# Attention and a gated MLP in one kernel: nine score tiles a pair in three groups, the remainder tile transposed as one block, minimum and exponential over two banks

## The chip, the cores and the metric

The kernel runs on one core of a Trainium2 chip. The metric is the device time of one execution in microseconds (us), the median over runs. The core's engines are TensorE (PE in the rows; PEld is its weight load), VectorE (DVE), ScalarE (ACT), GpSimd (POOL) and SyncE (SP), which here only issues DMAs.

## The reference, cut to what matters

```python
q, k, v: (4, 8, 1152, 64) float32        # batch, heads, sequence, head size
q_pool = q.reshape(B, H, S // 2, 2, D).mean(axis=3)      # 576 queries a head
scores = matmul(q_pool, k.T) / sqrt(D)
scores = scores - max(scores); attn = exp(scores); attn = attn / (sum(attn) + 1e-9)
x = (attn @ v), heads side by side                        # (2304, 512)
g = x @ w_gate; out = (g * sigmoid(g) * (x @ w_val)) @ w_out    # hidden size 1536
```

The weights come as float64. Operands of products are split into a high and a low half (each exact in TensorE's fp32r form), so a product of two operands is taken in two or three parts.

## The kernel before, in words

The attention works on 16 pairs of heads, one after another, with the operands of a pair prepared one pair ahead. A head has 576 queries: four tiles of 128 (`QT`) and a remainder of 64 (`QR`). The remainders of a pair's two heads make one tile together, so a pair has nine score tiles (`NTILE`), each 128 queries by 1152 keys.

- **Scores** (`s_tile`, L411). A tile's keys come in three chunks of 384 columns. A chunk takes two products (L427; the remainder tile four, since its queries of both heads stand in one tile `qrt` with zeros in the other head's place) into one of four single banks `sc`. VectorE takes the minimum of the negated scores, the first chunk by a reduction (L433), the other two by `tensor_scalar` with an accumulator that starts from the chunk before (L435). ScalarE then takes three exponentials (L441), each with its sum, into `pn` (for the remainder tile `pnr`), and frees the bank.
- **Groups** (`group`, L526, and `unit`, L468). The exponentials are transposed on TensorE (L484), 128 keys by 128 queries at a time, so that the products with v contract over keys. Each head has two groups: its first two tiles (256 queries, two key chunks to a bank `pt`), and its last two with its 64 rows of the remainder tile (320 queries, one key chunk to a bank, the 64-row block first). The bank is split in a high and a low half: ScalarE casts (L499), VectorE subtracts (L503). In three of nine units of the second group the bank is copied out (L489, L491) and GpSimd does the split (L497, L503). Then come the products with v (L511), high and low, of 256 or 320 columns, into `po`. `evac` (L546) adds up the halves of the result.
- **Operands.** `prep` (L386) transposes the split k and q of the next pair (L393) and copies them out (L398, L400). Queries are needed as [high, low] and as [low, high]; the second is the first, moved across partitions by two DMAs of `swap` (L376): for head 0 (`qt0`), head 1 (`qt1`) and the remainder (`qrt`, one buffer).
- **Sums.** When all nine tiles of a pair have their sums, `total` (GpSimd) and `recip` (VectorE, L573) give the reciprocals `rc`; `spread` stores them to DRAM (`rs`, L581 and L582), and then loads them back, a copy in each of 64 rows (`rb`, L586). `norm` (L593) multiplies.

All DMAs of a pair are issued by SP, in one fixed order; an issue whose source isn't ready holds up those behind it. The order on every engine is laid down before the run: `Plan` (L78) takes instructions with a cost, a place in the program (in units of a score tile) and the buffers that they take and give, and lists each engine's instructions by its own arithmetic, in which the places are shifted by a table of numbers (`SHIFTS`, L34). The chip then runs each engine's list in that order, with semaphores. The banks are `sc` 4, `pt` 3, `po` 1, which is all eight.

The MLP behind it takes blocks of 384 tokens; its weights are decoded from float64 by ScalarE, VectorE and GpSimd while the first two blocks run.

## Time and profile before

| what | value |
|---|---|
| three runs | 1144.87, 1134.54, 1147.23 us; median 1144.87 |
| the profiled execution | span 1150.8 us; no other time of it is listed |
| TensorE | 1078.2 us busy (94% of the span), 6369 products and transposes |
| VectorE | 724.6 us busy (63%) |
| ScalarE | 633.2 us busy (55%) |
| GpSimd | 415.5 us busy (36%) |
| first MLP product | 668.4 us from the span's start |

The table gives averages over two stages: the attention up to 668 us, and the MLP. What an edit of the attention is worth is read from the first stage alone. A TensorE product's busy time overlaps the next one's, so that what a product takes of the engine is the distance from its start to the next one's start, or its share in the chain of waits. The same holds for VectorE and ScalarE, whose rows overlap by some 0.1 us.

### The profile page before, as it was taken

Reading aid. Unit: us, or ns where it says so; the run is one execution under the profiler, and the core shown is the slowest. Engines: PE = TensorE matmul, PEld = TensorE weight load, DVE = VectorE, ACT = ScalarE, POOL = GpSimd, SP = SyncE. Lnnn points to the kernel's source line nnn. Section 1 sums busy time; section 2 is a strip of 40 time slices with the busy share of each in tenths; the row PEclk is TensorE's granted clock in tenths of the full one; section 3 lists DMA queues with packets and bytes.
Section 4 is the critical chain, followed back from the end, with each engine's and each line's share of the span. In section 5 each row is a group of like instructions: output and inputs, shape, how many; then the busy total and the mean of one; then the engine's idle time right before and its main releaser. Section 6 shows DMA issues by size and latency. Waiting matters only on the chain.

```text
span 1150.8 us, 18611 instructions
## 1 busy us (share of the span) xinstructions
PE 1078.2 (94%) x6369; PEld 955.8 (83%) x6369; DVE 724.6 (63%) x1618; ACT 633.2 (55%) x1710; POOL 415.5 (36%) x494
## 2 busy tenths in 40 slices
PE   6989999999999999999999988889999999999997
PEld 4878887787888888778788877778999999999997
DVE  7877876777777787677777859997332322322221
ACT  6867877777787787777778844443121121211211
POOL 7465446646447644644643244442110100100000
PEclk9999999999999999999999999999999999999999
DMA  6333134223224213312312024441020110100101
GB/s 219 106 103 80 49 106 122 40 80 97 56 61 133 77 32 105 96 37 80 77 35 34 22 76 146 147 146 38 28 83 1 28 29 1 55 1 1 28 1 28
DMA packets 68478, 77.17 MB, mean 67 GB/s; under 512 B 24032, under 2 KB 44384, under 8 KB 68384
## 3 DMA queue, kind: packets, MB, share of 16 engines
q1 hardware_dynamic: 68208, 75.59, 23.8%
q8 instruction: 50, 0.82, 0.3%
q14 instruction: 44, 0.36, 0.2%
q0 software_dynamic: 96, 0.26, 0.1%
q10 hardware_dynamic: 80, 0.13, 0.0%
HBM read 56.62 MB, written 9.51 MB: 57 GB/s over the span
## 4 chain that ended last, share of the span: by engine, by line
PE 72%; DVE 11%; ACT 6%; DMA 6%; issue 4%; SPq 0%; POOL 0%; POOLq 0%; DVEq 0%; ACTq 0%
PE pg L770 20%; PE pt L484 16%; PE sc L427 14%; PE po L511 10%; PE pa L792 10%; ACT pn L441 3%; DMA qrt<-qrt 3%; DVE wa L240 3%; PE pt L393 2%; DVE junk L435 2%; DVE w L244 2%; ACT ph L499 1%; DVE wa L236 1%; DVE sg L778 1%; DVE pl L503 1%
## 5 line engine op out<-in xcount | busy, mean ns | idle before, releaser
L770 PE MATMUL pg<-x,wh 128*128 128x384 f32 x1152 | 295.3, 337 | 0.0
L441 ACT ACTIVATE pn<-sc,mx 128x384 f32<-128x384 f32 x384 | 225.1, 591 | 4.6 <-DVE junk L435 3.1
L435 DVE TENSOR_SCALAR_CACHE_REDUCE junk<-sc,mx 128x384 f32<-128x384 f32 x288 | 177.6, 617 | 74.7 <-PE sc L427 65.3
L427 PE MATMUL sc<-kt,qt 128*128 128x384 f32 x768 | 213.6, 363 | 7.2 <-ACT pn L441 7.1
L484 PE MATMUL pt<-ident,pn 128*128 128x128 f32 x1152 | 215.0, 292 | 3.0 <-DVE pl L503 3.0
L770 PEld LDWEIGHTS pg<-x,wh 128*128 128x128 f32 x1152 | 208.8, 188 | 5.7
L770 PE MATMUL pg<-x,wl 128*128 128x384 f32 x576 | 194.8, 338 | 19.0 <-DVE sg L778 18.8
L778 DVE TENSOR_TENSOR sg<-pg,sg 128x384 f32<-128x384 f32 x144 | 80.0, 556 | 208.8 <-ACT sg L775 124.2
L503 DVE TENSOR_TENSOR pl<-pt,ph 128x320 fp32r<-128x320 f32 (+2 forms) x352 | 191.4, 551 | 8.5 <-ACT ph L499 7.3
L499 ACT CAST ph<-pt 128x320 fp32r<-128x320 f32 (+2 forms) x352 | 166.5, 483 | 47.7 <-PE pt L484 41.1
L511 PE MATMUL po<-ph,vs 128*128 128x256 f32 (+1 forms) x576 | 180.3, 326 | 0.0
L511 PE MATMUL po<-pl,vs 128*128 128x256 f32 (+1 forms) x576 | 164.6, 299 | 0.0
L484 PEld LDWEIGHTS pt<-ident,pn 128*128 128x128 f32 x1152 | 133.1, 144 | 27.1 <-DVE pl L503 2.5
L770 PEld LDWEIGHTS pg<-x,wl 128*128 128x128 f32 x576 | 108.7, 189 | 32.1 <-DVE sg L778 14.8
L427 PEld LDWEIGHTS sc<-kt,qt 128*128 128x128 f32 x768 | 120.7, 191 | 13.2 <-ACT pn L441 12.3
L782 ACT CAST hh<-sg 128x384 fp32r<-128x384 f32 x72 | 36.9, 513 | 152.3 <-PE pa L792 137.7
L511 PEld LDWEIGHTS po<-ph,vs 128*128 128x128 f32 x576 | 110.6, 192 | 1.0
L511 PEld LDWEIGHTS po<-pl,vs 128*128 128x128 f32 x576 | 111.1, 193 | 0.3 <-DVE pl L503 0.3
L433 DVE TENSOR_REDUCE mx<-sc 128x1 f32<-128x384 f32 x144 | 79.5, 552 | 49.3 <-PE sc L427 44.9
L775 ACT ACTIVATE sg<-pg 128x384 f32<-128x384 f32 x72 | 35.3, 490 | 126.3 <-PE pg L770 121.8
L427 PE MATMUL sc<-kt,qrt 128*128 128x384 f32 x192 | 57.1, 433 | 31.0 <-DMA qrt<-qrt 30.0
L792 PE MATMUL pa<-wh,hh 128*128 128x512 f32 x216 | 85.7, 397 | 0.0
(72 smaller groups left out, 1537.6 us busy)
## 6 DMA issues: line engine op xcount, KB each, us to landing
vraw<-in_v_dram SPq DMA_DIRECT2D x16, 576.0 KB
kraw<-in_k_dram SPq DMA_DIRECT2D x15, 576.0 KB
qraw<-in_q_dram SPq DMA_DIRECT2D x15, 512.0 KB
qt<-qt SPq DMA_DIRECT2D x60, 128.0 KB
wraw<-in_moe_w_out_dram SPq DMA_DIRECT2D x12, 512.0 KB
wraw<-in_moe_w_val_dram SPq DMA_DIRECT2D x12, 512.0 KB
wraw<-in_moe_w_gate_dram SPq DMA_DIRECT2D x12, 512.0 KB
rb<-rs SPq DMA_DIRECT2D x32, 144.0 KB
```

The source lines that it names most:

```text
L427: nc.tensor.matmul(cell[n][:, 0:KW], lhsT=lhsT, rhs=s[f"kt{jj}"][:, n * KW:(n + 1) * KW], start=(m == 0), stop=(m == len(terms) - 1))
L433: nc.vector.tensor_reduce(mx[:, 0:1], src, axis=AX.X, op=ALU.min)
L435: nc.vector.tensor_scalar(junk, src, mx[:, n - 1:n], None, op0=ALU.min, op1=ALU.min, accum_out=mx[:, n:n + 1])
L441: nc.scalar.activation(s["p", i][:, n * KW:(n + 1) * KW], cell[n][:, 0:KW], AF.Exp, bias=cell["mx"][:, 2:3], scale=-1.0, accum_out=s["sums ...
L484: nc.tensor.transpose(cell["ps"][:, o:o + r], s["p", i][r0:r0 + r, c * P:(c + 1) * P], ident[r0:r0 + r, r0:r0 + r])
L499: nc.scalar.copy(cell["h"][:, 0:w], cell["ps"][:, 0:w])
L503: e.tensor_sub(cell["l"][:, 0:w], cell["f" if kind else "ps"][:, 0:w], cell["h"][:, 0:w])
L511: nc.tensor.matmul(o[:, 0:n], lhsT=s["vs"][:, j, c, :], rhs=cell[x][:, a * n:(a + 1) * n], start=(first and a == 0 and x == "h"), stop=(en ...
L770: nc.tensor.matmul(o[:, 0:TB], lhsT=a[:, i, ws], rhs=b, start=(n == 0), stop=(n == 3 * NC - 1))
L778: nc.vector.tensor_mul(cell["s"], cell[i][:, 0:TB], cell["s"])
L782: nc.scalar.copy(cell["h"], cell["s"])
L792: nc.tensor.matmul(acc[blk, t], lhsT=cell[a][:, t * P:(t + 1) * P], rhs=b[:, 2, :], start=(f == 0 and n == 0), stop=(f == NF - 1 and n == 2),)
```

## The change

The score tile's three single banks become a bank pair `sa` (chunks 0 and 1, one slot) and a single bank `sb` (chunk 2, two slots). Chunk 2's products come first and are reduced; then chunks 0 and 1 are filled, and one VectorE instruction takes the minimum of both, and one ScalarE instruction their exponential; a second, short exponential follows for chunk 2. The nine tiles are taken in three groups of three: three of head 0; head 0's last, the remainder tile and one of head 1; three of head 1. A unit is one key chunk of a group, three transposes into one bank of 384 columns. In the middle group the remainder tile is transposed whole, and its two heads' 64 columns are written to two places in the bank, so that each head's 192 columns lie side by side; the products with v are then two pairs of 192 columns there, and one pair of 384 in the other groups. GpSimd takes no more part in the split. `Plan` has new costs for TensorE, and the table of shifts is new. In the changed kernel L431 are the score products, L488 the transposes of exponentials, L390 those of operands, L504 the products with v, L439 the two-bank minimum, L447 the exponentials, L373 the swaps, L563 and L564 the store and L568 the spreading of the reciprocals.

```diff
-        banks = {"sc": 4, "pt": 3, "po": 1}
+        banks = {"sa": 1, "sb": 2, "pt": 3, "po": 1}
...
-            "pn": 6, "pnr": 2, "ph": 5, "xs": 1, "tmp": 1, "pf": 2, "rb": 1, "xf": 1, "sums": 2, "rc": 2, "mx": 4,
+            "pn": 8, "ph": 5, "xs": 1, "tmp": 1, "rb": 1, "xf": 1, "sums": 2, "rc": 2, "mx": 4,
...
-            t = op({"PE": 0.056 * n}, pos, tr, after=after, take=("pt", *take), give=give, load=-1)
+            t = op({"PE": 0.065 * n}, pos, tr, after=after, take=("pt", *take), give=give, load=-1)
...
-            return (None, None) if i == QT else (1, i - QT - 1)
+            return (None, None) if i == QT else (1, (i - QT - 2) % QT)
...
             def mms(n):
+                if n == 2:
+                    cell["mx"] = new("mx", [P, 2], F32)
+                    cell["b"] = bank("sb", [P, 512])
                 if n == 0:
-                    cell["mx"] = new("mx", [P, 3], F32)
-                cell[n] = bank("sc", [P, 512])
+                    cell["a"] = bank("sa", [P, 2, 512])
+                o = cell["b"] if n == 2 else cell["a"][:, n]
...
             def low(n):
-                mx, src = cell["mx"], cell[n][:, 0:KW]
+                mx = cell["mx"]
                 if n == 0:
-                    nc.vector.tensor_reduce(mx[:, 0:1], src, axis=AX.X, op=ALU.min)
+                    nc.vector.tensor_reduce(mx[:, 0:1], cell["b"][:, 0:KW], axis=AX.X, op=ALU.min)
                 else:
-                    nc.vector.tensor_scalar(junk, src, mx[:, n - 1:n], None, op0=ALU.min, op1=ALU.min, accum_out=mx[:, n:n + 1])
+                    nc.vector.tensor_scalar(junk, cell["a"][:, :, 0:KW], mx[:, 0:1], None, op0=ALU.min, op1=ALU.min, accum_out=mx[:, 1:2])
 
             def exp(n):
...
                 nc.scalar.activation(
-                    s["p", i][:, n * KW:(n + 1) * KW], cell[n][:, 0:KW], AF.Exp, bias=cell["mx"][:, 2:3], scale=-1.0,
-                    accum_out=s["sums"][:, n, i:i + 1],
+                    o[:, 0:2 * KW].rearrange("p (a k) -> p a k", a=2) if n == 0 else o[:, 2 * KW:S],
+                    cell["a"][:, :, 0:KW] if n == 0 else cell["b"][:, 0:KW], AF.Exp, bias=cell["mx"][:, 1:2], scale=-1.0,
+                    accum_out=s["sums"][:, n, c:c + 1],
                 )
...
+            w = 0.175 * len(terms)
+            a, x = None, None
+            after = [*ready[2], *([done["s", p, m] for m in range(i)] if give else [])]
+            a = op({"PE": w}, pos - 0.3, lambda: mms(2), after=after, take=("sb", "mx"), load=1)
+            x = op({"DVE": 0.47}, pos - 0.25, lambda: low(0), after=[a])
+            a = op({"PE": w}, pos, lambda: mms(0), after=[a, *ready[0]], take=("sa",), load=1)
+            a = op({"PE": w}, pos + 0.01, lambda: mms(1), after=[a, *ready[1]], give=give, load=1)
+            x = op({"DVE": 0.95}, pos + LOW_AT, lambda: low(1), after=[a, x], more=0.04)
+            done["s", p, i] = a
+            x = op({"ACT": 0.88}, pos + EXP_AT, lambda: exp(0), after=[x], take=("pn", "sums") if i == 0 else ("pn",), give=("sa",))
+            done["p", p, i] = op({"ACT": 0.56}, pos + EXP_AT + 0.01, lambda: exp(1), after=[x], give=("sb", "mx"))
...
+        GROUPS = [
+            ([(0, None), (1, None), (2, None)], [(0, 0, 3 * P, 0)]),
+            ([(3, 0), (4, None), (5, P + QR)], [(0, 0, P + QR, 3 * P), (1, P + QR, 2 * (P + QR), 3 * P)]),
+            ([(6, None), (7, None), (8, None)], [(1, 0, 3 * P, 0)]),
+        ]
+        GW = 3 * P
...
+                for m, (i, o) in enumerate(tiles):
+                    src = s["p", i][:, c * P:(c + 1) * P]
+                    if i == QT:
+                        dst = cell["ps"][:, 0:GW].rearrange("p (a n) -> p a n", a=2)[:, :, P:P + QR]
+                        nc.tensor.transpose(dst, src, ident.rearrange("p (a n) -> p a n", a=2))
+                    else:
+                        o = m * P if o is None else o
+                        nc.tensor.transpose(cell["ps"][:, o:o + P], src, ident)
...
+                for n, (j, c0, c1, _) in enumerate(heads):
                     for x in ("h", "l"):
                         nc.tensor.matmul(
-                            o[:, 0:n], lhsT=s["vs"][:, j, c, :], rhs=cell[x][:, a * n:(a + 1) * n],
-                            start=(first and a == 0 and x == "h"), stop=(end and a == len(cs) - 1 and x == "l"),
+                            o[:, c0:c1], lhsT=s["vs"][:, j, c, :], rhs=cell[x][:, c0:c1],
+                            start=(c == 0 and n == 0 and x == "h"), stop=(c == KC - 1 and x == "l"), skip_group_check=len(heads) > 1,
                         )
...
+            a = op({"PE": 0.33}, pos, tr, after=[done["p", p, i] for i, _ in tiles], take=("pt",), load=-1)
+            b = op({"ACT": 0.37}, pos + HI_AT, hi, after=[a], take=("ph",))
+            x = op({"DVE": 0.468}, pos + LO_AT, lo, after=[b], give=("pt",))
+            return a, x, pv, 0.355 if len(heads) == 1 else 0.38
...
-            nc.gpsimd.tensor_add(r, s["sums"][:, 0], s["sums"][:, 1])
-            nc.gpsimd.tensor_scalar(r, r, 1.0, 1e-9, op0=ALU.mult, op1=ALU.add)
-            nc.gpsimd.tensor_add(r, r, s["sums"][:, 2])
+            nc.gpsimd.tensor_scalar(r, s["sums"][:, 0], 1.0, 1e-9, op0=ALU.mult, op1=ALU.add)
+            nc.gpsimd.tensor_add(r, r, s["sums"][:, 1])
...
-            for j in range(2):
-                for g in range(2):
-                    group(p, j, g, z + 4.5 * j + (0.0 if g == 0 else 2.05), 2.05 if g == 0 else 2.45)
+            for g in range(3):
+                group(p, g, z + 3.0 * g, 3.0)
...
-            a0 = op({"PE": 1.94}, s, lambda: gate(0), after=[wdone[0], *split_done.get(blk, [])], take=("pg0",))
+            a0 = op({"PE": 2.11}, s, lambda: gate(0), after=[wdone[0], *split_done.get(blk, [])], take=("pg0",))
```

The table of shifts moves instructions, which the diff doesn't show. On SP, the transfers between a pair's head 0 queries and the next pair's loads (`rs` and `rb` belong to the pair that ends, `qt0`, `qrt` and `qt1` to the next one); before:

```order
L376 DMA qt0_3525<-qt0_3525 64x512 x2
L581 DMA rs5_66<-rc_3658 128x4x1 x2
L582 DMA rs5_66<-rc_3658 2x64x1
L586 DMA rb_3763<-rs5_66 64x576 x2
L376 DMA qrt_106<-qrt_106 64x256 x2
L376 DMA qt1_3806<-qt1_3806 64x512 x2
L299 DMA kraw_3898<-in_k_dram 128x2x576
L303 DMA qraw_3938<-in_q_dram 128x2x512
L308 DMA qraw_3938<-in_q_dram 64x128 x2
```

and now:

```order
L373 DMA qt0_3189<-qt0_3189 64x512 x2
L373 DMA qrt_106<-qrt_106 64x256 x2
L563 DMA rs5_66<-rc_3315 128x4x1 x2
L564 DMA rs5_66<-rc_3315 2x64x1
L568 DMA rb_3441<-rs5_66 64x576 x2
L373 DMA qt1_3435<-qt1_3435 64x512 x2
L296 DMA kraw_3499<-in_k_dram 128x2x576
L300 DMA qraw_3523<-in_q_dram 128x2x512
L305 DMA qraw_3523<-in_q_dram 64x128 x2
```

The remainder's swap now stands ahead of the store and the spreading; head 1's swap still stands behind them.

On TensorE, around the score products of one tile in the middle of a pair (`sc`, `sa`, `sb` scores; `pt` from `pn`, `pnr` transposes of exponentials; `po` products with v); before:

```order
L427 MATMUL sc_4308<-kt0_3965,qt0_4109 128x384 x2
L484 MATMUL pt_4312<-ident_92,pnr_3947 128x64
L484 MATMUL pt_4312<-ident_92,pn_4202 128x128
L484 MATMUL pt_4312<-ident_92,pn_4133 128x128
L393 MATMUL pt_4317<-identr_97,ks_3739 128x128
L427 MATMUL sc_4326<-kt0_3965,qt0_4109 128x384 x2
L511 MATMUL po_4333<-ph_4283,vs_3312 128x320
L511 MATMUL po_4333<-pl_4284,vs_3312 128x320
L484 MATMUL pt_4337<-ident_92,pnr_3947 128x64
L484 MATMUL pt_4337<-ident_92,pn_4202 128x128
L484 MATMUL pt_4337<-ident_92,pn_4133 128x128
L511 MATMUL po_4333<-ph_4255,vs_3312 128x320
```

and now, from one fill of the bank pair to the next tile's single bank:

```order
L431 MATMUL sa_3614<-kt1_3364,qt1_3435 128x384 x4
L488 MATMUL pt_3625<-ident_92,pn_3347 128x128
L488 MATMUL pt_3625<-ident_92,pn_3412 128x128
L488 MATMUL pt_3625<-ident_92,pn_3467 128x128
L488 MATMUL pt_3631<-ident_92,pn_3347 128x128
L488 MATMUL pt_3631<-ident_92,pn_3412 128x128
L488 MATMUL pt_3631<-ident_92,pn_3467 128x128
L504 MATMUL po_3594<-ph_3584,vs_3041 128x384
L504 MATMUL po_3594<-pl_3585,vs_3041 128x384
L431 MATMUL sb_3644<-kt1_3364,qt1_3435 128x384 x2
L504 MATMUL po_3594<-ph_3591,vs_3041 128x384
L504 MATMUL po_3594<-pl_3592,vs_3041 128x384
```

A chunk's two products stood between sets of a 64-row block and two full tiles; now four products fill the bank pair together, and sets of three full tiles and pairs of 384 columns stand between.

## Rows read from the trace of the kernel before

**Rows 1.** The waits of PE from 60 to 640 us: who waited for whom, us in total, times, longest

```profile
PE sc L427 <- DMA qrt<-qrt: 30.0, 13, 3.3
```

**Rows 2.** Windows: busy us of each engine (instructions), granted clock, DMA share, GB/s

```profile
300.00:350.00 50.00, 47.59 (x309) 41.19 (x309) 37.68 (x96) 39.65 (x119) 27.97 (x35) 0.97 0.24 62
...
700.00:750.00 50.00, 43.38 (x220) 38.10 (x219) 48.90 (x76) 22.47 (x42) 20.18 (x14) 1.00 0.43 139
```

**Rows 3.** The chain of waits, 318 to 332 us: start, us, engine, line, times

```profile
318.04 0.29 PE pt L393 x4
...
319.59 0.71 PE po L511 x6
...
323.02 0.57 PE pt L484 x3
...
323.59 0.29 PE po L511 x2
...
327.30 0.35 PE sc L427 x2
...
329.73 0.44 PE pt L484 x4
```

**Rows 4.** The timeline of PE, a run of four transposes: start, us, instruction

```profile
329.57 0.60 PE L484 MATMUL pt<-ident,pn 128*128 128x128 f32 x4
...
329.92 0.60 PE L427 MATMUL sc<-kt,qt 128*128 128x384 f32 x2
...
330.35 0.31 PE L511 MATMUL po<-ph,vs 128*128 128x320 f32 x1
```

**Rows 5.** The timeline of SP's queue, one pair: start, us of issuing, transfer

```profile
296.80 0.92 SPq L581 DMA_DIRECT2D rs<-rc  x2
...
306.60 1.39 SPq L586 DMA_DIRECT2D rb<-rs  x2
...
308.10 1.15 SPq L376 DMA_DIRECT2D qrt<-qrt  x2
...
337.86 1.24 SPq L581 DMA_DIRECT2D rs<-rc  x2
```

**Rows 6.** The timeline of ACT, the copy of the remainder queries

```profile
304.29 0.34 ACT L398 ACTIVATE qrt<-pt 128x64 fp32r<-128x64 f32 x2
```

**Rows 7.** The timeline of PE, the remainder's first products [idle before, released by]

```profile
311.89 1.44 PE L427 MATMUL sc<-kt,qrt 128*128 128x384 f32 x4 [2.23 <-DMA qrt<-qrt]
```

**Rows 8.** Windows of 1 us behind that wait, first and last slow one

```profile
312.00:313.00 1.00, 1.00 (x4) 1.00 (x5) 0.00 (x0) 0.00 (x0) 0.00 (x0) 0.55 0.70 203
...
315.00:316.00 1.00, 1.00 (x8) 1.00 (x7) 0.67 (x3) 0.57 (x3) 1.00 (x2) 0.74 0.00 0
```

**Rows 9.** The timeline of DVE, subtractions of 320 and 512 columns, minima

```profile
325.39 0.48 DVE L503 TENSOR_TENSOR pl<-pt,ph 128x320 fp32r<-128x320 f32 x1
...
325.80 0.55 DVE L433 TENSOR_REDUCE mx<-sc 128x1 f32<-128x384 f32 x1
...
332.48 0.69 DVE L503 TENSOR_TENSOR pl<-pt,ph 128x512 fp32r<-128x512 f32 x1
...
333.08 0.61 DVE L435 TENSOR_SCALAR_CACHE_REDUCE junk<-sc,mx 128x384 f32<-128x384 f32 x1
...
333.62 0.69 DVE L503 TENSOR_TENSOR pl<-pt,ph 128x512 fp32r<-128x512 f32 x1
```

**Rows 10.** Groups by line and form, ACT's casts: xcount, busy us, mean ns

```profile
L499 ACT CAST ph<-pt 128x320 fp32r<-128x320 f32 x192 | 81.6, 426 | 38.6 <-PE pt L484 32.9 <-PE sc L427 2.0 <-POOL pl L503 0.4
...
L499 ACT CAST ph<-pt 128x512 fp32r<-128x512 f32 x128 | 74.4, 595 | 8.7 <-PE pt L484 7.7 <-PE sc L427 0.2
```

**Rows 11.** The timeline of ACT, an exponential that frees a bank

```profile
334.39 0.58 ACT L441 ACTIVATE pn<-sc,mx 128x384 f32<-128x384 f32 x1
...
334.87 0.20 ACT L441 ACTIVATION_READ_ACCUMULATOR pn<-sc,mx 128x1 f32 x1
```

**Rows 12.** The timeline of PE, the score products that waited for it

```profile
335.12 0.62 PE L427 MATMUL sc<-kt,qt 128*128 128x384 f32 x2 [0.17 <-ACT pn L441]
```

More of the change, by code (lines that the diff above doesn't have):

```diff
@@ L64 @@
     "first": (
[L65 removed]
+        "AP.P.A.P.PPA..P.DPDPPA.DADAA.AA."
     ),
     "pair": (
[L68 removed]
+        "DDADA..A."
     ),
@@ L443, in exp @@
-                    accum_out=s["sums"][:, n, i:i + 1],
-                )
-            w = 0.162 * len(terms)
-            pn = "pnr" if i == QT else "pn"
-            a, b = None, None
-            for n in range(3):
-                after = [a, *ready[n]]
-                if n == 2:
-                    after += [done["s", p, m] for m in range(i) if give]
-                a = op({"PE": w}, pos + 0.3 * n, lambda n=n: mms(n), after=after, take=("sc", "mx") if n == 0 else ("sc",), give=give if n == 2 else (), load=1)
-                b = op({"DVE": 0.53 if n else 0.465}, pos + 0.3 * n + LOW_AT, lambda n=n: low(n), after=[a, b], more=0.04)
@@ L455, in s_tile @@
-            for n in range(3):
-                take = ((pn, "sums") if i == 0 else (pn,)) if n == 0 else ()
-                b = op({"ACT": 0.56}, pos + EXP_AT + 0.01 * n, lambda n=n: exp(n), after=[b], take=take, give=("sc", "mx") if n == 2 else ("sc",))
-                done["s", p, i] = a
-            done["p", p, i] = b
-        def group_tiles(j, g):
-            base = 0 if j == 0 else QT + 1
-            if g == 0:
-                return [(base, 0, P), (base + 1, 0, P)]
-            return [(base + 2, 0, P), (base + 3, 0, P), (QT, j * QR, QR)]
@@ L472, in unit @@
[L472 to L473 removed]
+            tiles, heads = GROUPS[g]
             cell = {}
[L475 removed]
             def tr():
                 cell["ps"] = bank("pt", [P, 512])
[L479 to L484 removed]
@@ L536, in group @@
             x = None
-            for u, (pos, _, c, pv, us) in enumerate(made):
-                end = u == len(made) - 1
-                give = ("ph", "vs") if end and j == 1 and g == 1 else ("ph",)
+            for c, (_, after, pv, us) in enumerate(made):
+                end = c == KC - 1
                 x = op(
-                    {"PE": us}, pos, lambda pv=pv, u=u, end=end: pv(u == 0, end), after=[c, x, done["v", p, j]],
-                    take=("po",) if u == 0 else (), give=give, load=1,
-                )
@@ L544, in group @@
-            evac(p, j, g, made[-1][0] + 0.01, x)
-        def evac(p, j, g, pos, after):
+                    {"PE": us}, w0 + wd * c / KC + PV_LAG, pv, after=[after, x, *(done["v", p, j] for j, *_ in GROUPS[g][1])],
+                    take=("po",) if c == 0 else (), give=("ph", "vs") if end and g == 2 else ("ph",), load=1,
+                )
+            pos = w0 + wd + PV_LAG
+            heads = GROUPS[g][1]
+            for n, h in enumerate(heads):
+                evac(p, g, *h, pos + 0.02 * n, x, n == len(heads) - 1)
@@ L547, in evac @@
+        def evac(p, g, j, a0, a1, c0, pos, after, last):
             s = st[p]
-            n = sum(r for _, _, r in group_tiles(j, g))
-            c0 = 0 if g == 0 else 2 * P
+            n = a1 - a0
             main, corr = (slice(0, D), slice(D, P)) if j == 0 else (slice(D, P), slice(0, D))
@@ L553, in cp @@
             def cp():
[L554 to L555 removed]
+                cell["t"] = new("tmp", [P, GW], F32)
+                nc.scalar.copy(cell["t"][main, 0:n], s["o", g][corr, a0:a1])
             def add():
[L558 to L560 removed]
+                nc.vector.tensor_add(made(s, "xs", [P, SP], F32)[main, c0:c0 + n], s["o", g][main, a0:a1], cell["t"][main, 0:n])
             added = done.setdefault(("xs", p), [])
[L562 removed]
+            a = op({"ACT": n / 1200 + 0.05}, pos, cp, after=[after], take=("tmp",))
+            x = op({"DVE": n / 960 + 0.068}, pos + 0.01, add, after=[a, *added], take=("xs",) if g == 0 else (), give=("tmp", "po") if last else ("tmp",), more=0.08)
             added.append(x)
```

131 lines of the change are left out of this document (44 added, 87 removed).

## The prediction

> **What bounds the kernel now.** I read the waits first, then the windows, then the chain. From 60 to 640 us TensorE's one wait of any size is thirteen times for the swapped remainder queries [rows 1]; in a window of that stage it is busy 47.6 of 50 us, VectorE 37.7 and ScalarE 39.7 [rows 2]. So the attention is bound by TensorE, with room on the others. From 700 to 750 us VectorE is full (48.9 of 50) [rows 2]: there it decodes weights, which the change doesn't touch.
>
> A pair takes 41.06 us (from one reciprocals' store to the next, 296.80 to 337.86) [rows 5]. The chain prices TensorE's work in it [rows 3]: 60 score products at 0.35 a two, 10.5 us; 36 value products of 256 columns at 0.71 a six and 36 of 320 at 0.29 a two, 9.5; 27 operand transposes at 0.29 a four, 2.0. The exponentials' transposes come in 18 sets of one 64-row block and two full tiles, 0.57 each, and ten runs of full tiles. Four full ones cost 0.35 until the next product starts, so 0.0875 each, and that product's pair then takes 0.43 where the chain has 0.35: a changeover of about 0.09 [rows 4]. With it a four is the chain's 0.44 and a two 0.26. That is 10.3 + 8 x 0.44 + 2 x 0.26 = 14.3 us. The sum is 36.3.
>
> The other 4.8 us: the wait, 2.2 [rows 7]; behind it four windows of 1 us with a granted clock of 0.55, 0.50, 0.50 and 0.74 [rows 8], that is partly at 1.2 GHz, which cost 0.45 + 0.5 + 0.5 + 0.26 = 1.7 (twelve of the thirteen waits have such a tail); 0.9 for small waits. The wait's cause stands on SP: ScalarE's copy of the remainder queries is done at 304.63 [rows 6], but their swap is issued at 308.10, behind the spreading of the reciprocals, which stood until 306.60 for the store issued at 296.80 to land [rows 5].
>
> **Transposes.** All 18 sets with a 64-row block go. 27 sets of three full tiles come: 81 x 0.0875 = 7.1 us, and in the new order 17 changeovers a pair, 1.5: 8.6 against 14.3. Nine of the sets write the remainder in two blocks of 64 columns, which no row shows: its set costs from 0.35 (three full tiles and a changeover) to the old set's 0.57; I take the low end, since the slow set differs in rows read, not only in columns written.
>
> **Value products.** 36 of 384 columns, 0.175 each as the score products [rows 3], and 36 of 192, 0.095 each, between operand transposes of 128 columns (0.073) and products of 256 (0.118) [rows 3]: 6.3 + 3.4 = 9.7 us, up 0.2; the ends give 8.9 to 10.5. The Trainium skill's page "TensorE: Matmul & The Clock Gate" (section "LDWEIGHTS") gives 107 ns for loading 128 columns of weights; if that were a floor, 36 x 0.012 = 0.4 us a pair or 6 us in all would be added. The operand transposes load new weights each and come every 73 ns [rows 3], so the trace doesn't bear it out as a floor.
>
> TensorE's sum falls from 36.3 to 30.8 us a pair.
>
> **The remainder's wait.** The new SP order has the swap of the remainder queries ahead of the store and the spreading, and 10.5 us of TensorE work, where 5.5 stood, lie between their transpose and their use. The 2.2 and 1.7 us go. What is late next is head 1's query swap, which now stands behind the spreading. The store waits for the pair's last tile: from its first product into the bank pair 3.1 us to the end of the long exponential (the loop below), 1.0 for a cast and the short one, and an estimated 1.8 for two small GpSimd operations, the reciprocal and what stands ahead of it: 5.9. By rows 5 the transfer behind the spreading is issued 11.3 us after the store (308.10 - 296.80), and its data are used 3.8 us after that [rows 5, 7]: 21.0. The new order has 19.1 us of TensorE work between the same product and the first product with those queries (40 score products, 7.0 us; 51 transposes, 4.5; 18 wide and 24 narrow value products, 5.4; 19 operand transposes and nine changeovers, 2.2). Short by 1.9, less what TensorE has waited in between: I take 1.1, and 0.85 for a slow clock behind half of such waits.
>
> **The two-bank tile.** One bank pair holds chunks 0 and 1, and the next tile's products into it wait until the exponential has read it. The loop: four products, 0.62 for two from start to finish behind a wait [rows 12] and 0.35 more, 0.97; VectorE's minimum over 768 columns, 0.61 [rows 9] and 0.40 for 384 columns more, 1.01 (from 320 to 512 columns a subtraction takes from 0.41 to 0.60 of the engine [rows 9], about 1 ns a column); ScalarE's exponential, 0.58 and the sum's reading until 0.68 [rows 11], and 0.34 more at the casts' 0.88 ns a column (595 - 426 over 192) [rows 10], 1.02; three hand-overs of 0.05 [rows 11, 12]. Sum 3.15 us; nine tiles and four more products for the remainder make 29.1 us a pair. That is under TensorE's 30.8, by 0.2 us a tile only.
>
> **VectorE.** It gets the sixth of the subtractions that GpSimd did: 27 x 0.475 = 12.8; minima over one bank 9 x 0.47 = 4.2 and over two 9 x 0.94 = 8.5 (0.54 from one start to the next [rows 9], and 0.40); three operand copies at 0.60, 1.8; output sums and reciprocal, 1.7. Sum 29.0 of 30.8: 94%, where it was some 75% by the window [rows 2]. ScalarE loses nine exponentials of 27, and its sum falls. GpSimd loses work for which TensorE had no wait of any size.
>
> So three things need 29.0, 29.1 and 30.8 us, in one fixed order. The old small waits (0.9) stay, and I add 0.85 a pair for the bank loop behind a subtraction. 30.8 + 0.9 + 0.85 + 1.1 + 0.85 = 34.5 us a pair.
>
> **Sum.** Fifteen distances between 16 pairs, 15 x 6.56 = 98 us. The start and the 10.5 us behind the last scores (10.7 in the new order) I cost at nothing, the MLP too: TensorE's order there is the same but for three products at the end; VectorE's and ScalarE's are shifted during decoding, a few us either way. The profiled span is 1150.8 us and gives 1052; it lies 6 us over the median of the three runs, 1144.87, so the median should be 1046.
>
> **Rivals.**
> - No new wait: head 1's queries land in time and the loop fits the order, as the sums just allow. 32.3 us a pair, 131 us less: 1014. Against it: both fit by less than 0.2 us a tile or not at all. Chance 0.17.
> - Queueing in the loop: one subtraction (0.47) ahead of most minima and half a short exponential ahead of most long ones, 3.9 us a tile, 35.9 a pair, and 1.1 for the query wait: 37. 61 us less: 1084. The 94% speaks for it; that the waited-for instructions stand spaced out by two to five others speaks against. Chance 0.20.
> - The remainder's two-block set stays at the old 0.57: 9 x 0.22 = 2.0 us a pair, and 36.5: 1076. The Trainium skill's page "PSUM — Partial Sum Buffer" (Specifications) says that any non-contiguous access pattern slows matmuls significantly; the rows of before have contiguous outputs only, so the trace neither bears it out nor speaks against it. Chance 0.06.
> - Slower: every hand-over of the loop finds a foreign instruction ahead, a subtraction (0.47), the other exponential (0.58), a set of transposes and a product pair (0.70). 4.9 us a tile, 44.8 a pair, 56 us more: 1201. It decides from (41.06 - 0.7) / 9 = 4.48 us a tile. Before, four single banks let TensorE run ahead; now one slot doesn't. Chance 0.06.
>
> My forecast has 0.50 with its own range of 1028 to 1066 (1.2 us a pair each way, the size of the query wait); 0.01 is left for no change. About 1% is what a measurement can tell from none. Faster: 0.93; within 1%: 0.01; slower: 0.06. The range of 1008 to 1092 takes in the forecast, most of the first rival and the next two.
>
> **What would show it.** After: no set of transposes over 0.40 us; no wait of TensorE for the remainder's swap, a wait of 1 to 2 us a pair for head 1's query swap, SP standing at the spreading; the score products waiting for the exponential a few tenths a tile; VectorE busy over 85% of a window. A pair of over 36 us with score products waiting over 0.5 us a tile would say that the loop is the bound and that I priced queueing too low; a set at 0.57 that the two-block output is; no wait for head 1's queries that the store lands faster than before.

## The result, and the profile after

The changed kernel takes 1110.08 us, the median of 1112.77, 1110.77, 1102.18 and 1109.39; beside it the kernel before took 1142.65, the median of four. The ratio is 0.969, with a 95% interval of 0.962 to 0.976. That is faster, but a third of the gain forecast, and above the range's upper end of 1092. The profiled execution has a span of 1111.0 us where before had 1150.8: 39.8 us less, where the sum had 98.4.

The attention gained 50.7 us (its end, the first MLP product, moved from 668.4 to 617.7 us) and the MLP lost 10.9 (from there to the span's end, 482.4 to 493.3). A pair, from one reciprocals' store to the next, takes 37.13 us in the mean of 15 distances, where it took 40.59, and 34.5 was forecast.

Waits of TensorE, 60 to 600 us (who for whom: us in total, times, longest), the answer to [rows 1]:

```profile
PE sb L431 <- DMA qt<-qt: 30.8, 13, 5.8
PE sb L431 <- ACT pn L447: 2.4, 2, 2.0
PE sb L431 <- DMA qrt<-qrt: 1.6, 1, 1.6
PE pt L488 <- DVE pl L496: 0.6, 1, 0.6
```

The remainder's wait has gone and one of the same size has come for head 1's queries. (The 2.0 us put down to ScalarE stand at the same product of another pair, 4.5 us behind the swap's issue like the others, so they are probably the swap's too.) For the bank pair the list has one wait, of 0.3 us. The cause of the new wait is the one forecast; SP's queue, one pair (start, us of issuing, transfer), against [rows 5]:

```profile
281.99 0.57 SPq L373 DMA_DIRECT2D qrt<-qrt  x1
282.66 1.11 SPq L563 DMA_DIRECT2D rs<-rc  x2
283.83 0.55 SPq L564 DMA_DIRECT2D rs<-rc  x1
292.32 1.13 SPq L568 DMA_DIRECT2D rb<-rs  x2
293.54 1.55 SPq L373 DMA_DIRECT2D qt<-qt  x2
```

The swap is issued 10.9 us after the store, behind a spreading that stood until the store had landed. Two whole pairs as windows (busy us of PE, PEld, DVE, ACT, POOL with instructions, then the granted clock, DMA share, GB/s), and two windows against [rows 2]:

```profile
300.00:350.00 50.00, 47.54 (x332) 44.35 (x330) 41.24 (x85) 38.76 (x101) 20.67 (x23) 0.97 0.36 103
700.00:750.00 50.00, 39.78 (x199) 34.55 (x198) 44.49 (x68) 20.09 (x37) 18.63 (x13) 1.00 0.34 106
245.59:282.66 37.07, 35.20 (x243) 33.03 (x242) 30.38 (x63) 28.63 (x75) 13.47 (x14) 0.95 0.34 83
282.66:317.78 35.12, 33.74 (x243) 31.36 (x242) 30.25 (x63) 28.51 (x75) 13.49 (x14) 1.00 0.35 88
```

The first of the two pairs has a wait of 1.8 us for the queries, the second one of 1.3. Without the wait they take 35.3 and 33.8: the 1.5 us between them are the clock, which behind the first wait falls to 0.50 (windows of 1 us, same columns; the granted clock is 1.00 before and after the slow ones):

```profile
261.40:262.40 1.00, 1.00 (x6) 1.00 (x7) 0.38 (x1) 0.66 (x4) 1.00 (x2) 1.00 1.00 334
262.40:263.40 1.00, 1.00 (x8) 0.97 (x6) 1.00 (x3) 0.00 (x0) 0.92 (x2) 0.76 1.00 361
263.40:264.40 1.00, 1.00 (x5) 1.00 (x4) 0.11 (x1) 0.48 (x1) 0.66 (x1) 0.50 0.84 288
264.40:265.40 1.00, 1.00 (x6) 0.90 (x6) 0.41 (x1) 0.00 (x0) 0.00 (x0) 0.50 0.77 227
265.40:266.40 1.00, 1.00 (x6) 1.00 (x6) 1.00 (x3) 0.56 (x2) 0.00 (x0) 0.53 0.80 228
```

So in nine of the 15 pairs, within 0.1 us, a pair is 33.8 us of TensorE's work, plus its wait, plus 1.5 where the clock falls; the first three and the last two lie outside this, and one has another wait. TensorE's timeline in the middle group (start, us, instruction):

```profile
304.08 0.27 PE L488 MATMUL pt<-ident,pn 128*128 128x128 f32 x1
304.19 0.27 PE L485 MATMUL pt<-ident,pn 128*128 128x128 f32 x1
304.30 0.38 PE L488 MATMUL pt<-ident,pn 128*128 128x128 f32 x2
...
308.40 0.27 PE L504 MATMUL po<-pl,vs 128*128 128x192 f32 x1
308.51 0.28 PE L504 MATMUL po<-ph,vs 128*128 128x192 f32 x1
308.62 0.27 PE L504 MATMUL po<-pl,vs 128*128 128x192 f32 x1
```

L485 is the remainder's transpose into two blocks: it takes 0.11 us like its neighbours. The products of 192 columns come 0.11 apart, where I had 0.095.

### The profile page after: what moved, and what is told of

It reads as the page before. It is cut to its first block, busy times and chain, and to the rows that moved or that the text cites. A ratio compares the mean times of both kernels' runs of the same rounds, so it can differ in the third digit from the quotient of the medians.

```text
span 1111.0 us, 17417 instructions
## 1 busy us (share of the span) xinstructions
PE 1022.3 (92%) x6225; PEld 945.2 (85%) x6225; DVE 720.2 (65%) x1378; ACT 586.8 (53%) x1424; POOL 295.4 (27%) x300
## 4 chain that ended last, share of the span: by engine, by line
PE 62%; DVE 12%; ACT 10%; DMA 7%; issue 6%; SPq 2%; POOL 1%; POOLq 0%; ACTq 0%; DVEq 0%
PE pg L748 21%; PE pa L770 11%; PE po L504 10%; PE pt L488 8%; PE sa L431 6%; ACT pn L447 5%; PE sb L431 4%; DMA qt<-qt 4%; ACT ph L493 4%; DVE wa L237 3%; DVE w L241 2%; PE pt L390 2%; DVE junk L439 2%; DVE pl L496 1%; DVE wa L233 1%
## 5 line engine op out<-in xcount | busy, mean ns | idle before, releaser
L493 ACT CAST ph<-pt 128x384 fp32r<-128x384 f32 x432 | 197.8, 487 | 124.5 <-PE pt L488 100.0
L496 DVE TENSOR_TENSOR pl<-pt,ph 128x384 fp32r<-128x384 f32 x432 | 230.1, 552 | 43.0 <-ACT ph L493 35.3
L748 PE MATMUL pg<-x,wl 128*128 128x384 f32 x576 | 195.1, 339 | 29.0 <-DVE sg L756 28.9
L488 PE MATMUL pt<-ident,pn 128*128 128x128 f32 x1152 | 196.1, 283 | 3.3 <-DVE pl L496 1.6
L504 PE MATMUL po<-ph,vs 128*128 128x384 f32 (+1 forms) x576 | 181.0, 329 | 0.1
L504 PE MATMUL po<-pl,vs 128*128 128x384 f32 (+1 forms) x576 | 172.4, 314 | 0.6 <-DVE pl L496 0.6
L439 DVE TENSOR_SCALAR_CACHE_REDUCE junk<-sa,mx 128x768 f32<-128x768 f32 x144 | 145.7, 1012 | 34.0 <-PE sa L431 32.8
L488 PEld LDWEIGHTS pt<-ident,pn 128*128 128x128 f32 x1152 | 143.6, 144 | 27.1 <-DVE pl L496 7.2
L431 PE MATMUL sa<-kt,qt 128*128 128x384 f32 x512 | 132.4, 365 | 5.5 <-ACT pn L447 5.5
L447 ACT ACTIVATE pn<-sa,mx 128x768 f32<-128x768 f32 x144 | 132.1, 918 | 9.8 <-DVE junk L439 9.3
L760 ACT CAST hh<-sg 128x384 fp32r<-128x384 f32 x72 | 36.9, 513 | 165.4 <-PE pa L770 145.3
L504 PEld LDWEIGHTS po<-pl,vs 128*128 128x128 f32 x576 | 112.5, 195 | 1.5 <-DVE pl L496 1.4
L504 PEld LDWEIGHTS po<-ph,vs 128*128 128x128 f32 x576 | 112.2, 195 | 1.0 <-issue 0.4
L431 PE MATMUL sb<-kt,qt 128*128 128x384 f32 x256 | 73.8, 371 | 33.3 <-DMA qt<-qt 30.8
L437 DVE TENSOR_REDUCE mx<-sb 128x1 f32<-128x384 f32 x144 | 79.3, 551 | 27.6 <-PE sb L431 27.1
L431 PEld LDWEIGHTS sa<-kt,qt 128*128 128x128 f32 x512 | 87.1, 198 | 9.4 <-ACT pn L447 7.1
```

The costliest lines, as they stand in the source:

```text
L431: nc.tensor.matmul(o[:, 0:KW], lhsT=lhsT, rhs=s[f"kt{jj}"][:, n * KW:(n + 1) * KW], start=(m == 0), stop=(m == len(terms) - 1))
L437: nc.vector.tensor_reduce(mx[:, 0:1], cell["b"][:, 0:KW], axis=AX.X, op=ALU.min)
L439: nc.vector.tensor_scalar(junk, cell["a"][:, :, 0:KW], mx[:, 0:1], None, op0=ALU.min, op1=ALU.min, accum_out=mx[:, 1:2])
L447: nc.scalar.activation(o[:, 0:2 * KW].rearrange("p (a k) -> p a k", a=2) if n == 0 else o[:, 2 * KW:S], cell["a"][:, :, 0:KW] if n == 0 el ...
L488: nc.tensor.transpose(cell["ps"][:, o:o + P], src, ident)
L493: nc.scalar.copy(cell["h"], cell["ps"][:, 0:GW])
```

## The experiments

Each batch ran on one chip beside the kernel before, and chips differ (before took 1143 to 1163 us), so kernels are compared by their ratio to it or by stages of their profiles. A pair is the median of the 15 distances from one store of reciprocals to the next, the MLP stage runs from its first product to the span's end.

| kernel | ratio to before [95%] | pair, us | MLP stage, us |
|---|---|---|---|
| before | 1 | 40.94 | 482.4 |
| changed | 0.969 [0.962, 0.976] | 37.07 | 493.3 |
| after_again | 0.971 [0.967, 0.975] | 38.43 | 493.5 |
| swap_first | 0.925 [0.922, 0.928] | 34.08 | 493.5 |
| old_mlp_costs | 0.966 [0.963, 0.969] | 37.87 | 486.5 |
| both | 0.918 [0.916, 0.921] | 34.08 | 486.5 |
| before_swap_first | 0.955 [0.952, 0.958] | 37.14 | 482.9 |
| before_light | 0.958 [0.955, 0.962] | 37.41 | 483.1 |
| one_bank_ops | 0.962 [0.960, 0.964] | 37.18 | 486.7 |
| light_minimum | 0.912 [0.910, 0.915] | 33.51 | 486.2 |
| sg_apart | 0.918 [0.916, 0.920] | 34.06 | 481.2 |
| best | 0.913 [0.912, 0.915] | 34.07 | 481.0 |
| best2 | 0.910 [0.907, 0.913] | 34.05 | 481.3 |
| narrow_half | 0.919 [0.911, 0.928] | 34.06 | 479.7 |

**swap_first.** The planner is told that the store takes longer, which moves the spreading behind the swap on SP:

```diff
-            y = op({"SP": 1.7}, ..., lambda p=p: spread(p, 0), after=[y], give=("rc",), more=2.1)
+            y = op({"SP": 1.7}, ..., lambda p=p: spread(p, 0), after=[y], give=("rc",), more=6.0)
```

> The changed kernel with one difference on SP alone: in the pairs where it stood behind it, head 1's query swap goes ahead of the spreading of the reciprocals (13 places; the other engines' orders are the same). Theory (the spreading, which stands until the store has landed, makes the swap late, and the slow clock behind the wait costs as much again): TensorE's waits for that swap, 30.8 us in the changed kernel, fall under 5 us, the granted clock stays near 1.00, a pair takes 33.5 to 34.5 us in place of 37.1, and the span falls by 40 to 55 us, to 1056 to 1071. Rival A (the two-bank loop or VectorE is the bound, and the wait only hid it): the wait goes, but score products wait for the exponential in its place, pairs stay at 35 us or more, and less than 25 us is gained. Rival B (the swap is late since its queries' transposes or their copy are late, not by its place on SP): the waits stay above 20 us in all and the time within 1%.

The theory holds, at the lower end of its range in the span (39.8 us less, 1071.2). SP's queue, one pair, and TensorE's window:

```profile
298.44 1.12 SPq L563 DMA_DIRECT2D rs<-rc  x2
299.61 0.55 SPq L564 DMA_DIRECT2D rs<-rc  x1
303.32 1.13 SPq L373 DMA_DIRECT2D qt<-qt  x2
310.31 1.10 SPq L568 DMA_DIRECT2D rb<-rs  x2
```

```profile
300.00:350.00 50.00, 49.82 (x345) 45.41 (x344) 43.87 (x90) 41.52 (x110) 31.45 (x34) 1.00 0.42 112
```

The swap goes out 4.9 us after the store; of the waits for queries 3.4 us are left in the first pair, where the order is the old one, and 2.0 near the end; behind the first pair the clock stands at 1.00, and 15 pairs take 517.3 us where they took 557.0: 39.7 us for one place on a queue. These two profiles come from two chips. On one chip the same edit lies between `old_mlp_costs` and `both` below: the 15 pairs go from 576.5 to 518.4 us, 58.1 less, since the waits there were longer to begin with. What the place costs thus varies with how late the store lands, while a pair without the wait takes 34.08 us in both. The spreading goes out 11.9 us after the store in place of 9.7; GpSimd's waits for it are 8.9 us in place of 7.7 (100 to 560 us), and TensorE has none from it.

**before_swap_first.** The kernel before with the same edit (`more=5.0` for pairs 1 to 13), which moves both late swaps ahead of the spreading.

> The kernel before with its own SP order changed alone: the swap of the remainder queries and the one of head 1's queries go ahead of the spreading (13 pairs). Theory (its 2.2 us wait and the 1.7 us of slow clock behind it are due to the place on SP alone): TensorE's 30.0 us of waits for the remainder's swap fall under 5, a pair goes from 40.6 to 36.5 to 37.5 us, and the kernel gains 40 to 55 us, so that more than the whole gain of the changed kernel is to be had without regrouping. Rival (the wait hid another, for VectorE, ScalarE or the banks, which takes its place): a pair stays at 39 us or more and less than 25 us is gained.

The theory holds (4.8 us of waits for the remainder's swap are left), and it tells what the regrouping is worth, by which I mean all of the change but the order on SP: the SP order alone gives 0.955, more than the whole change. Between this kernel and `both`, run on the same chip, the time falls from 1111.48 to 1068.11 us, with TensorE full in both (49.83 and 49.82 us busy from 300 to 350) and a pair going from 37.14 to 34.08. The regrouping saves 3.06 us a pair, not the 5.5 by which I had TensorE's sum fall; on this chip the SP order alone took 51.6 us off the kernel before, the regrouping another 43.4 with the planner's costs of the next run put right.

**old_mlp_costs.** The costs that only the planner reads:

```diff
-            a0 = op({"PE": 2.11}, s, lambda: gate(0), ...
+            a0 = op({"PE": 1.94}, s, lambda: gate(0), ...
...
-                    {"PE": 0.69}, s + 1.65 + 0.1 * t, lambda t=t: proj(t), ...
+                    {"PE": 0.64}, s + 1.65 + 0.1 * t, lambda t=t: proj(t), ...
```

> The changed kernel with the planner's two costs of the MLP's products as they were before (1.94 and 0.64 in place of 2.11 and 0.69): the attention's orders are the same, TensorE's order in the MLP too, only VectorE's, ScalarE's and GpSimd's order there differs. Theory (the new costs place VectorE's products with the gate later among the weights' decoding, and TensorE waits for them): the MLP's stage goes from 493 us back to about 482, TensorE's waits for VectorE's gate from 28.9 back to about 19, and the kernel gains 8 to 12 us. Rival (the MLP lost its time to something that the attention leaves behind, such as the state of the decoded weights or of x when it starts): the stage stays at 490 us or more, and the time within 3 us.

The theory holds in part: the MLP's stage falls by 6.8 us of the 10.9, TensorE's waits for the gate from 28.9 to 22.6, where I had 482 and 19. The gain in the total is not resolved from run to run (0.966 and 0.969), since the attention of this chip waited longer for the queries (38.7 us in 12 waits). That the new costs, through the order that they give, cost the 6.8 us is shown, and 6.3 of it appears as TensorE's waits for VectorE's product with the gate; 4 remain. **both** has the two edits together.

> Both edits together. Theory: they lie in different stages and add up, 48 to 67 us less than the changed kernel, a span of 1044 to 1063. Rival (a faster attention moves the weights' first decoding or the loads for the MLP against each other): the sum falls short by 10 us or more.

They add up: attention 577.9 us, as in swap_first, and MLP 486.5, as in old_mlp_costs. The span of 1064.4 is 46.6 us below the changed kernel's, just short of the 48 forecast, because old_mlp_costs had given 6.8 us where I had 8 to 12.

**sg_apart.** For the other 4 us, ScalarE where the MLP begins (start, us, instruction [idle before, released by]); in the kernel before:

```profile
668.62 0.42 ACT L555 COPY tmp<-po 64x320 f32<-64x320 f32 x1 [1.33 <-PE po L511]
670.75 1.28 ACT L775 ACT_TABLE_LOAD   x1 [1.71 <-PE pg L770]
676.53 0.49 ACT L775 ACTIVATE sg<-pg 128x384 f32<-128x384 f32 x1 [4.50 <-POOL xf L593]
```

and in the changed one:

```profile
617.92 0.47 ACT L538 COPY tmp<-po 64x384 f32<-64x384 f32 x1 [1.29 <-PE po L504]
628.41 1.28 ACT L753 ACT_TABLE_LOAD   x1 [10.01 <-DMA xd<-xf]
629.70 0.49 ACT L753 ACTIVATE sg<-pg 128x384 f32<-128x384 f32 x1
```

The MLP's first tile `sg` lies in memory that the attention used. Before, it waited until GpSimd had read the pair's last output; now, with other sizes in the pool, until the store of that output has landed, and the table load waits as well. The edit gives `sg` a place of its own:

```diff
-                cell["s"] = new("sg", [P, TB], F32)
+                cell["s"] = stage.tile([P, TB], F32, name="sg", tag="sg", bufs=2)
```

> The kernel of both edits with the MLP's gate tile sg in a pool that is reserved from the start, so that it shares no memory with the attention's last output tile. Theory (in the changed kernel the first sigmoid and its table load of 1.28 us wait 10 us for the store of that tile to land, which they did not before; this is the 4 us of the MLP's loss that the planner's costs don't explain): the table load comes right behind the first gate's products, TensorE's longest wait there falls from 9.0 us to 2 or 3, and the MLP's stage from 486.5 to 479 to 483 us: 4 to 7 us less. Rival (another tile of the MLP then lies there, or the weights are late as well): the wait moves behind and the time stays within 2 us.

```profile
577.05 1.28 ACT L753 ACT_TABLE_LOAD   x1
578.65 0.49 ACT L753 ACTIVATE sg<-pg 128x384 f32<-128x384 f32 x1 [0.31 <-PE pg L748]
...
587.45 0.51 ACT L760 CAST hh<-sg 128x384 fp32r<-128x384 f32 x1 [5.89 <-DMA xd<-xf]
```

In the profile the stage falls by 5.3 us to 481.2, and the next tile, `hh`, waits for the same store. The stage is now 1.2 us shorter than in the kernel before, so the two causes, 6.8 and 5.3, are a little more than the 10.9 lost. The ratio, taken on another chip than that of `both`, doesn't resolve the 5 us. **best2** is best with `hh` apart in the same way.

> As best, and the MLP's tile hh apart from the attention's memory too. Theory (behind the sigmoid, the first cast into hh waits for the same store, and TensorE 2.9 us for it): that wait goes, 2 to 4 us less than best, a ratio to before of 0.910 to 0.912. Rival (hl or the weights' tiles lie there as well): no change beyond 1 us.

The rival holds: TensorE now waits 3.2 us for `hl`, and the stage stays at 481.3.

**best** is sg_apart with the swap ahead in the first pair too (`more=8.0` there).

> As sg_apart, and head 1's query swap ahead of the spreading in the first pair too (with a load and one of GpSimd's instructions that change places there). Theory: the first pair's waits of 3.1 and 2.0 us and the slow clock behind them go, 41.1 us become about 35: 5 to 7 us less than sg_apart, a span of 1050 to 1055. Rival (in the first pair the queries themselves come late from GpSimd, which prepares them): the swap is issued no earlier and the pair stays at 40 us or more.

The first pair falls from 41.1 to 35.9 us, as the theory has it, but the second rises from 33.5 to 36.0: the 15 pairs take 3.6 us less, and the span 3.5. On one chip with sg_apart its median is 1055.46 against 1061.01. With best2 it is the fastest complete kernel here, 0.91 of before and some 6% below the changed kernel.

**light_minimum** asks what holds TensorE at 34.08:

```diff
-                    nc.vector.tensor_scalar(junk, cell["a"][:, :, 0:KW], mx[:, 0:1], ...
+                    nc.vector.tensor_scalar(junk[:, :, 0:8], cell["a"][:, :, 0:8], mx[:, 0:1], ...
```

> The kernel of both edits, in which the minimum over the bank pair reads and writes 8 columns of each bank in place of 384 (it leaves out most of the maximum; the exponentials take what minimum they get). VectorE's instruction falls from 1.01 us to about 0.3, so the loop of the bank pair shortens by some 0.7 us a tile and VectorE's work by 6 us a pair. Theory (TensorE's own work is the bound, 33.9 of 34 us busy, and I priced its transposes, narrow products and operand transposes too low): a pair stays at 34.1 us, within 0.3, and the time within 1% of the kernel of both edits (0.918 of before). Rival (the one-slot bank loop or VectorE's queue spaces TensorE's instructions out, without a wait that the records list): a pair falls by 1 us or more, the time by 15 us or more.

Between the two: a pair falls by 0.57 us. VectorE has lost 8 of 44 us in the window and TensorE is as full as before, so at most 33.5 is TensorE's own, and 0.6 came from the loop or VectorE's queue, which the run relieves together:

```profile
300.00:350.00 50.00, 49.91 (x356) 47.42 (x355) 36.07 (x94) 41.33 (x108) 27.49 (x29) 1.00 0.45 126
```

**one_bank_ops** undoes one part of the change:

```diff
-                    nc.vector.tensor_scalar(junk, cell["a"][:, :, 0:KW], ...
+                    for a in range(2):
+                        nc.vector.tensor_scalar(junk[:, a], cell["a"][:, a, 0:KW], ...
...
+                for a in (0, 1) if n == 0 else (2,):
+                    nc.scalar.activation(o[:, a * KW:(a + 1) * KW], cell["a"][:, a, 0:KW] ...
```

> The kernel of both edits with one part of the change undone: the minimum and the exponential over the bank pair each split again into one instruction a bank (9 more minima and 9 more exponentials a pair, in the same places of the same orders; the groups, the transposes and the bank pair stay). The loop of the bank pair grows by about 0.25 us a tile on VectorE and 0.2 on ScalarE, from 3.15 to some 3.6, which is 32.4 + 0.4 us a pair with the remainder. Theory (TensorE's work bounds the pair with 34.1): a pair grows by less than 0.7 us, the kernel by less than 10 us, so that the gain of the regrouping lies in the transposes alone. Rival (the loop has no room left): a pair grows by 2 us or more, the kernel by 30 us or more, and the two-bank instructions are what makes the regrouping possible.

My theory fell, the rival holds: a pair takes 3.1 us more, 0.34 a tile, most of the 0.45 by which the loop was to grow. TensorE now has waits of which the other regrouped kernels list 0.2 to 0.6 us at most (60 to 600 us; the window below):

```profile
PE sa L431 <- ACT pn L449: 6.6, 27, 0.5
PE pt L489 <- DVE kt L397: 5.0, 13, 0.4
PE pt L489 <- DVE pl L497: 3.0, 13, 0.2
```

```profile
300.00:350.00 50.00, 47.47 (x322) 41.86 (x321) 43.84 (x112) 41.99 (x126) 21.50 (x25) 1.00 0.38 106
```

The timeline shows the loop closing: the next fill of the bank pair starts 0.05 us after the last exponential of the one before has ended.

```profile
316.69 0.20 ACT L449 ACTIVATION_READ_ACCUMULATOR pn<-sa,mx 128x1 f32 x1
316.94 0.61 PE L431 MATMUL sa<-kt,qt 128*128 128x384 f32 x2
```

From 300 to 375 us all 18 fills start within 0.06 us of that end; in `both`, from 300 to 370, 4 of 19 do, and the others come 0.1 to 0.6 later. So the loop with one instruction a bank is the bound at 37.2; with 9 x 0.45 us less, the two-bank loop needs some 33 (an estimate from these two numbers), about what TensorE needs. I had it at 29.1.

**before_light** is before_swap_first with its second and third minimum on 8 columns.

> The kernel before with its swaps ahead of the spreading, in which the second and third minimum of a tile read and write 8 columns in place of 384 (it leaves out most of the maximum). Theory (with the old groups TensorE's 37 us a pair is the bound alone, so that lighter instructions on VectorE and ScalarE, which is the two-bank part of the change by itself, would give it nothing): a pair stays at 37.1 us within 0.5. Rival (the old kernel too was held by the tiles' loop): a pair falls by 1.5 us or more.

The old groups gain nothing from a lighter VectorE (0.958 against 0.955, TensorE at 49.83 of 50): there TensorE alone is the bound. So neither part gained anything without the other in the form that was run: the new groups with one-bank instructions take 37.2 us a pair, the old groups with a lighter minimum 37.4, and both parts together 34.1. Two forms were not run, and what they are worth is open: the two-bank instructions themselves on the old groups, and the new groups with the four single banks of before, where one-bank instructions would not have had to share one slot.

**after_again** is the changed kernel a second time, on another chip.

> The changed kernel, unedited, a second time with profile. Theory: TensorE's work without waits is the same in each pair, 33.8 us, each wait for head 1's queries adds its own length, and 1.5 us of slow clock where it is 1.8 us or longer; the MLP's stage is 493 us, 7 more than in the kernel with the planner's old costs. Pairs of 35 to 38 us and a span of 1105 to 1130 us, by how long the store takes to land. Rival (pairs differ for other reasons): pair minus wait scatters by more than 1 us at the same granted clock.

The waits for the queries are longer (37.95 us a pair in the mean, a ratio of 0.971). Pair minus wait comes in steps by the granted clock: 33.8 to 33.9 at 1.00, 35.3 to 35.5 in most pairs at 0.95 to 0.96, 36.2 to 36.9 at 0.91. Outside these lie the first pair and the last, and two with 34.4 and 34.5 at 0.96 and 0.95. These two, the third and the 14th, are some 1 us below the others, the scatter that the rival asked for; but they are short in swap_first too (33.5 us, where most take 34.1), so about half of it is in their own orders. The theory's 1.8 us fell: two pairs with waits of 2.0 and 1.9 us keep a mean clock of 1.00, as one with 2.35 us does in the kernel before. The length of the wait alone doesn't tell whether the clock falls, and what else does is open.

**narrow_half** asks what a narrow product costs; the middle group's products take 96 columns of 192 in eight of nine key chunks.

> The kernel best2, in which the products with v of the middle group take 96 columns in place of 192 in eight of nine key chunks (it leaves out half of those products). Theory (a narrow product costs what its weights take to load, 0.11 us, not what its columns take): two such products in a row still start 0.10 to 0.11 us apart, and a pair falls by less than 0.4 us. Rival (it costs by its columns, and the 0.11 has another cause): they start 0.08 us apart or less, and a pair falls by 0.8 us or more.

```profile
318.44 0.27 PE L504 MATMUL po<-pl,vs 128*128 128x96 f32 x1
318.55 0.27 PE L504 MATMUL po<-ph,vs 128*128 128x96 f32 x1
318.66 0.28 PE L504 MATMUL po<-pl,vs 128*128 128x96 f32 x1
```

Half the columns, and still 0.11 apart; the pair stays at 34.06. The loads of the weights are 0.11 apart too, each 0.05 us ahead of its product:

```profile
318.39 0.19 PEld L504 LDWEIGHTS po<-pl,vs 128*128 128x128 f32 x1
318.50 0.19 PEld L504 LDWEIGHTS po<-ph,vs 128*128 128x128 f32 x1
318.61 0.19 PEld L504 LDWEIGHTS po<-pl,vs 128*128 128x128 f32 x1
```

The product ahead of these three starts at 318.39, and the first of them starts only 0.05 us behind it: 96 columns need no more than that, and the 0.11 is the pace of the loads. The theory holds.

## Why the prediction was wrong, point by point

The profile gained 39.8 us in place of 98.4. The 58.6 us between them, by the steps of the sum:

| step | forecast | measured | us lost |
|---|---|---|---|
| TensorE's work and small waits, a pair | 30.8 + 0.9 + 0.85 = 32.55 | 33.8 | 18.8 |
| listed waits, a pair (queries, and the few others) | 1.1 | 2.4 | 20.0 |
| the rest, mostly slow clock, a pair | 0.85 | 0.9 | 0.7 |
| a pair before | 41.06 | 40.59 in the mean | 7.0 |
| MLP | 0 | +10.9 | 10.9 |
| start and end of the attention | 0 | +1.2 | 1.2 |

- **The remainder's wait** went, as forecast, and the late one next is head 1's swap behind the spreading, as forecast. The step that failed is its size: "Short by 1.9, less what TensorE has waited in between: I take 1.1". The waits came to 2.2 us a pair, from 0.6 to 5.8. That the 1.9 lies so near is luck, as both of its sides were too small. The 21.0 us were 22.8 in the pair shown: 10.9 from store to swap against 11.3, 4.4 from there to the product against 3.8, and 7.5 from the last tile's first product to the store where I had 5.9. In that last part GpSimd is done at 279.83, and the reciprocal starts 1.9 us later, behind a minimum and a subtraction on VectorE:

```profile
275.16 0.53 PE L431 MATMUL sa<-kt,qt 128*128 128x384 f32 x2
279.63 0.20 POOL L552 TENSOR_TENSOR rc<-rc,sums 128x9 f32<-128x9 f32 x1 [0.80 <-ACT pn L447]
281.74 0.20 DVE L555 RECIPROCAL rc<-rc 128x9 f32<-128x9 f32 x1
```

TensorE's work between the same two products took 21.5 us where I had 19.1. Pairs with longer waits have a later landing (13.0 us from store to swap in the one with 2.7). No row had a wait for the 0.8 that I subtracted. swap_first shows that this place on SP costs 39.7 us with its clock, 58.1 on another chip.

- **TensorE's sum** is the other: 5.5 us less a pair forecast, 3.06 measured between two kernels that TensorE fills (37.14 and 34.08). The old side was right in sum (36.3 and 0.9). The new side was short. Transposes: "0.0875 each" is the mean of a run of four [rows 4]; the rows of after below give 0.24 for three alone and 0.90 for nine, so 0.11 for each further one, and the new order has most of them in sixes and nines. With the changeovers, which lie in the products behind them, 81 of them took 10.5 us in swap_first where I had 8.6. Narrow products: 4.2 where I had 3.4. Operand transposes: 2.6 for 2.0, but they took 2.7 in before_swap_first too, so there they lay in my 0.9 of small waits. Of the 2.4 us between 5.5 and 3.06 the transposes thus have some 1.8 (3.9 us saved where I had 5.7) and the value products 0.8 (1.0 added where I had 0.2), an estimate with the score products at their old price. Some of this is small waits that the records don't list, for which I had 1.75. TensorE's timeline of the changed kernel (start, us, instruction):

```profile
254.04 1.14 PE L488 MATMUL pt<-ident,pn 128*128 128x128 f32 x9
254.94 0.42 PE L504 MATMUL po<-ph,vs 128*128 128x384 f32 x1
...
299.46 0.49 PE L488 MATMUL pt<-ident,pn 128*128 128x128 f32 x3
299.70 0.60 PE L431 MATMUL sa<-kt,qt 128*128 128x384 f32 x2
```

- **The weights' load.** The rows of before had operand transposes 73 ns apart, and I took it that there is no floor of 107 ns. narrow_half shows one for these products: 0.11 us with 192 columns and with 96, at the pace of their weights' loads. The Trainium skill's page "TensorE: Matmul & The Clock Gate" (section "LDWEIGHTS") has a load take its columns divided by 1.2 in ns, by which 128 columns are an estimated 107 ns. The trace agrees for these products; for operand transposes, 73 ns apart, it doesn't, and why they differ is open.
- **The two-block transposes** cost nothing extra (0.11 us, as their neighbours): that rival is out. The Trainium skill's page "PSUM — Partial Sum Buffer" (Specifications) has non-contiguous patterns slow matmuls significantly; with two runs of 64 columns this trace shows none of it.
- **The loop** was sized at 29.1 us a pair and needs some 33 by one_bank_ops: 0.4 us a tile more than the three durations and hand-overs, which I put down to queueing on VectorE and ScalarE (no run measured that by itself). Its price in the forecast (0.85) was near the measured 0.57 all the same, since TensorE's floor lay higher too. That loop and TensorE would lie close was right. That the changed kernel's 37.1 us a pair equal the queueing rival's 37 is chance: without the late swap it takes 34.1, so its loop was not the bound, and only one_bank_ops made it one. The slower rival is out.
- **VectorE**: its work is 30.2 us a pair where I had 29.0, and in swap_first it is busy 43.9 of 50 us, 88%, with TensorE's sum larger than forecast.
- **The MLP** "a few us either way": it was put at nothing without a look at either of its causes, and lost 10.9: 6.8 by planner costs that were raised, and the other 4 by a tile that came to share memory with a later store (5.3 when it was set apart). Neither can be read off the attention's lines of the diff.
- **One pair for fifteen**: 41.06 was a typical pair with its wait, but the second and third and the last two are shorter (36.9 to 40.1); the 15 distances were there to be added up.

## What to carry to other kernels

An in-order queue with a round trip through DRAM in it should have everything else that is due ahead of the return leg: here that one edit beat the regrouping. Where a price comes from a short run of instructions, read a long run before multiplying it, and price a product of few columns (192 here) by its weights' load, not by the columns. Where two resources come out within a few per cent of each other, a change that relieves one of them may look worthless until the other is relieved too; and when the sizes of a phase's buffers change, look at the first waits of the phase behind it.

## What the hardware showed that I had not expected

- In a row of products with v, one with 96 and one with 192 columns both take 0.11 us until the next starts; one of 384 takes 0.175.
- Three transposes of fp32 tiles by themselves take 0.24 us until the next product starts, nine take 0.90.
- A wait of 1.8 us for a transfer is followed some 1 us later by 4 us with a granted clock of 0.76 to 0.50, partly at 1.2 GHz, which adds 1.5 us; the pairs with waits of 0.6 to 1.6 us in the same profile keep 1.00, but so do single pairs with 1.9 to 2.35 us in after_again and in the kernel before.
- The store of 576 reciprocals a head, 4 bytes an element, keeps the load that reads them back, and what stands behind it on the queue, waiting for 7.9 us (from 284.38, where the store's issue ends, to 292.32).
